# Keys of batch 0 with tokens on partitions, outers from PSUM, beta on 48 rows, d_ff in quarters, and loads placed in the written order

## The chip, the cores and the metric

The kernel runs on one core of one Trainium2 chip. The metric is the device time of an execution in microseconds. A core has five engines that run their own instruction queues in order: TensorE (PE, matmuls, with weight loads listed apart as PEld), VectorE (DVE), ScalarE (ACT), GpSimd (POOL) and SyncE (SP, which here only issues DMAs). All times below are microseconds unless marked otherwise, and positions are counted from the start of the profiled span.

## The reference

Two stages. The first is an attention without softmax over batch 4, heads 4, sequence 1088, head size 32. Each query and key is projected by two 8x32 sketches, and the outer product of the two results is its 64-element feature. The second is a feed-forward layer of 2048 units over all 4352 tokens.

```
phi(x) = outer(S1 x, S2 x)                  # 8 x 8 = 64 features for each token and head
kv  = sum over s of phi(k_s) v_s^T          # 64 x 32 for each batch and head
z   = sum over s of phi(k_s)
x_s = (phi(q_s) kv) / (phi(q_s) z + 1e-6)   # heads side by side: 4352 x 128
h   = x w_in;  g = h * sigmoid(beta * h);  out = g w_out
```

## The kernel before, in words

**Order.** Nothing is scheduled by a planner. Each step is a small function with a short name, and the string `SEQ` lists the names in the order in which they are issued; each engine runs its own part of that list in order. A name in capitals puts the same step on the second engine of its pair (`o01` on GpSimd, `O01` on VectorE; `ca1` on ScalarE, `CA1` on VectorE). `+` issues one wave of the feed-forward layer (`w1`: two 512-column matmuls of xT with w_in units into a two-bank PSUM buffer `wave`, L384, and one silu on ScalarE, L393). `-` issues one accumulation (`w2`: two matmuls with scaled w_out units, L359). `~` is one warming matmul (`keep_warm`, L189) that computes nothing needed. Eleven more of these are issued at the very start. A chunk is 512 tokens and needs 8 waves and 8 accumulations; there are 68 of each in all, the last four with 256 columns in place of 512. `+` is issued only for tokens whose xT has been made.

**PSUM.** `wave` has two buffers of two banks, `two` one buffer of two banks, `one` one bank, and `moeout` one bank. Whoever wants a buffer waits for the last reader of the tile before.

**Batch 0 (the prologue).** k arrives in two loads, with head and 32 groups of tokens on partitions. VectorE turns it in 32x32 blocks (`turn_k`, L420). `kps` projects it with the sketches (L447, 8 matmuls of 288 columns), and `kab` turns the result, so that tokens lie on partitions (L468). `outer` multiplies the two projections to features (L483, in five pieces, `o00` to `o04`), `gram` (L545) with `gram_terms` and `gram_z` makes z, and `kv0` accumulates kv with v (L531). Of q, batch 0 is done in two parts: A (tokens 0 to 511, loaded first) and B (512 to 1087, a later load). `spread` projects q twice, as a (`aa`, `ab`) and b (`ba`, `bb`); `asb` copies a's result out of PSUM (`ca`, `cb`), `mult` multiplies it by b's (`ma`, `mb`). `den0` multiplies by z (`da`), `invert` and `spread_rc` make the reciprocals (`ia`, `ra0`, `ra1`), `num0` makes the numerator (`na`), and `divide0` writes xT (`xa0`, `xa1`, L624).

**Weights.** The silu needs beta times h, so w_in is multiplied by beta (`prep_win`, `u0` to `u3`, 512 columns each, on GpSimd, L308) and w_out divided by it (`prep_rbeta`, L316, and `prep_wout_act`, `w0` to `w7`, L322). beta is first split into three bf16 terms on 12 partitions (`beta_top`, `beta_left`) and broadcast by matmuls with a selector (`beta_half`, L283) and copies (`beta_copy`, L293). A d_ff index is half, partition and unit of eight, so unit j of a half is read from `winp` with a step of 8.

**Batches 1 to 3** follow among the waves: `tk`, `kp`, `ka`, outers, `g` (gram, L636), `gm`, `wz`, `qp`, `qa`, `c`, outers of q (`p10` ...) and their turns (`t10` ...), kv (`va`, `vb`), `np`, and the numerator (`n1`, L721).

**Loads.** All loads but three small ones go through SP's queue. In the kernel before they are issued ahead of everything: k 0, first q 0, v 0 (four loads of 144 KB), both halves of w_in, half of w_out, beta_pu (for `rb`), second q 0, k 1, the other half of w_out, q 1, v 1, k 2, q 2, v 2. At most eight are under way: the ninth after a load waits until that load has landed.

Of the kernel before, what the change touches and what calls it, by code (L numbers as in the profile page):

```python
# [9 lines left out]
F32 = mybir.dt.float32  # L10
# [4 lines left out]
P = 128  # L15
# [3 lines left out]
def kernel(  # L19
# [12 lines left out]
    nc = tc.nc  # L32
# [26 lines left out]
    NU = NJ // 2  # L59
# [25 lines left out]
    def sb(shape, dtype, name):  # L85
        return const.tile(shape, dtype, tag=name, name=name)
# [7 lines left out]
    beta_pu = sb([P, 2, NU], F32, "beta_pu")  # L94
    NB = 3 * 4
    beta_r = sb([NB, DFF // 4], F32, "beta_r")
# [3 lines left out]
    for n, s_ in enumerate((S1, S2)):  # L100
# [10 lines left out]
            ap=[[DFF // 4, 4], [0, 3], [1, DFF // 4]],  # L111
# [16 lines left out]


# [18 lines left out]
    def load_wout(i):  # L148
        nc.sync.dma_start(
            out=w_out_sb[:, NU * i : NU * i + NU, :],  # L150
            in_=bass.AP(
                tensor=moe_w_out.tensor,
                offset=moe_w_out.offset + i * NU * P * P,
                ap=[[NU * P, P], [1, NU * P]],
            ),
        )

    def load_late():
        nc.sync.dma_start(
            out=beta_pu,  # L160
            in_=bass.AP(
                tensor=moe_beta.tensor, offset=moe_beta.offset, ap=[[NU, P], [P * NU, 2], [1, NU]]
            ),
        )

    K_PARTS = ((0, 18), (18, T))
    QA0 = 2 * q_chk[0][1]
    load_rows(k, k_t, 0, "k", K_PARTS)
    load_rows(q, q_t, 0, "q", ((0, QA0),))
    load_v(0)  # L170
    load_win(0, DFF // 2)
    load_win(DFF // 2, DFF)
    load_wout(0)
    load_late()
    load_rows(q, q_t, 0, "q", ((QA0, T),))
    load_rows(k, k_t, 1, "k")
    load_wout(1)
    load_rows(q, q_t, 1, "q")
    load_v(1)
    load_rows(k, k_t, 2, "k")  # L180
    load_rows(q, q_t, 2, "q")
    load_v(2)

# [42 lines left out]
    for n in range(2):  # L226
        qT2.append(sb([P, T, 32], F32, f"qT{n}"))
        kT2.append(sb([P, TPAD, 32], F32, f"kT{n}"))
        nc.gpsimd.memset(kT2[n][:, T:, :], 0.0)
    zb0 = sb([P, H, 32], F32, "zb0")  # L230
# [5 lines left out]
    bsel = sb([NB, 4], BF16, "bsel")  # L236
    bsel4 = sb([NB, 4], F32, "bsel4")
    nc.vector.tensor_reduce(out=bsel4, in_=cut(ident[:NB], [[3, 4], [1, 3]]), op=ADD, axis=AX.X)
# [3 lines left out]
        out=bpos[:, 0:1], in_=cut(ident[:NB], [[3, 4], [1, 2]], 1), op=ADD, axis=AX.XY  # L242
    )
    nc.vector.tensor_reduce(
        out=bpos[:, 1:2], in_=cut(ident[:NB], [[3, 4]], 2), op=ADD, axis=AX.X
# [9 lines left out]
    skc = sk.rearrange("p m n r -> p (m n r)")  # L255
    sab = []


    def prep_s(n):
        st_ = sb([P, 4, R], F32, f"st{n}")  # L260
        nc.vector.transpose(out=st_.rearrange("p u r -> p (u r)"), in_=sr[n])
        nc.gpsimd.tensor_tensor(out=sk[:, :, n, :], in0=st_[:, :2, :], in1=hm, op=MUL)
        t = sb([P, R, R], F32, f"s{n}")
        nc.scalar.copy(out=t, in_=cut(st_, ([[1, R], [0, R]], [[0, R], [1, R]])[n]))
        sab.append(t.rearrange("p i j -> p (i j)"))
# [4 lines left out]
    bq = sb([NB, DFF // 4], BF16, "bq")  # L270
    br = [beta_r, sb([NB, DFF // 4], F32, "br1"), bq]
    bt = sb([NB, DFF // 4], BF16, "bt")
# [7 lines left out]
    def beta_half(i):  # L280
        t = two("betaps")
        for n in range(2):
            nc.tensor.matmul(  # L283
                out=t[:, n],
                lhsT=cut(bsel, [[0, P]], 2 * i + n),
                rhs=bq,
                start=True,
                stop=True,
            )
        PS["beta", i] = t  # L290

    def beta_copy(i):
        nc.scalar.copy(  # L293
            out=beta_bc[:, 1024 * i : 1024 * i + 1024],
            in_=PS["beta", i].rearrange("p a b -> p (a b)"),
        )
# [6 lines left out]
    WP = 512  # L303
# [6 lines left out]
    def win_unit(j):  # L310
        i, u = divmod(j, NU)
        assert all(n in given for n in range(i * NU * P // WP, (i + 1) * NU * P // WP))
        return cut(winp, [[NU, P]], i * NU * P + u)
# [110 lines left out]

    def turn_q(b, t0=0, t1=T):
        nc.vector.transpose(  # L426
            out=qT2[b % 2][:, t0:t1].rearrange("p t s -> p (t s)"),
            in_=q_t[b][:, t0:t1].rearrange("p t d -> p (t d)"),
        )

    PS, KP, QO, QT, QP, ND, KAB, QAB, ASB, KVZ, KVD, RB = ({} for _ in range(12))
# [32 lines left out]

    def turn_ab(t, name):
        o = sbA.tile([P, NJK, H, 2 * R], F32, tag=name, name=name)
        for pi in range(2):
            nc.vector.transpose(out=cut(o, [[2 * R * H, NJK], [1, 32]], 32 * pi), in_=t[:, pi, :JW])  # L468
        return o
# [8 lines left out]
    def outer(dst, b, src, nm, j0, j1, eng=None):  # L478
        if b not in dst:
            dst[b] = sbA.tile([P, NJK, H, F], F32, tag=nm, name=nm, bufs=1)  # L480
        a0 = src[b][:, j0:j1]
        n = H * (j1 - j0)
        (eng or nc.vector).tensor_tensor(  # L483
            out=cut(dst[b][:, j0:j1], [[F, n], [R, R], [1, R]]),
            in0=cut(a0, [[2 * R, n], [1, R], [0, R]]),
            in1=cut(a0, [[2 * R, n], [0, R], [1, R]], R),
            op=MUL,
        )
# [11 lines left out]
    def spread(which, n, dsts):  # L500
        t0, tn = q_chk[n]
        for c in range(2):
            for m in range(2):
                for pr, dst in enumerate(dsts):
# [3 lines left out]
                        out=dst[64 * c : 64 * c + 64, m, : 32 * tn],  # L508
# [231 lines left out]
    def b_A():  # L740
        PS["bA"] = [wave2("bps"), wave2("bps")]
        spread("b", 0, PS["bA"])
# [86 lines left out]
    do("kp0", kps, 0)  # L829
    do("ka0", kab, 0)  # L830
# [23 lines left out]
    for n in range(2):  # L854
        do(f"s{n}", prep_s, n)
        do(f"tk0{n}", turn_k, 0, *K_PARTS[n])
        do(f"be{n}", beta_half, n)
        do(f"bc{n}", beta_copy, n)
# [9 lines left out]
    for n in range(DFF // WP):  # L868
        do2(f"u{n}", prep_win, (n,), POOL, DVE)
    for i in range(NJ // 2):  # L870
        do(f"w{i}", lambda i: [prep_wout_act(j) for j in (2 * i, 2 * i + 1)], i)
    for b in range(1, B):
# [41 lines left out]
        s1 s0 sw bt0 ~ bl0 ~ ~ tk00 tk01 ~ kp0 bt1 tqa aa ca0 ~ ka0 ~ BL1 gr zt ~ o00 ca1 be0 ba o01 ~  # L914
        bc0 O02 ma0 zz v00 ma1 o03 be1 o04 lk3 da ia v01 bc1 v02 v03 ra1 v04 rb kd u1 nd nc u0 ra0 tqb
        na ~ w0 w2 ab w3 cb0 xa0 xa1 u3 + CB1 w1 bb ~ tk1 mb1 ~ + - kp1 w6 + mb0 ka1 u2 + O11 - w7 g1 -
        o12 w4 + tq1 + gm1 wz1 qp1 wm1 db w5 - + nb qa1 c1 ib o13 o10 xb + - - ct1 + CM1 cr1 CD1 - P11 +
        p12 - + va1 t12 p13 vb1 vc1 + p10 + np1 - t11 + - nz1 - - lq3 t13 t10 + n1 x10 tk2 x11 - + kp2 +
        - ka2 - + o23 tq2 - + g2 + lv3 - gm2 wz2 - o21 o22 tk3 wm2 + + c2 qp2 o20 + - + qa2 ct2 CM2 - +
        - - + cr2 - CD2 p21 P20 + - + va2 vb2 t21 + VC2 - + - p22 np2 nz2 t22 - p23 t20 t23 + n2 x20 x21  # L920
        - tq3 + kp3 ka3 O30 + - + - + g3 + gm3 wz3 - o32 + o33 - wm3 + qp3 qa3 + c3 + - + - - + - + ct3
        CM3 o31 cr3 - CD3 + va3 P33 p32 vb3 P30 vc3 + - t33 p31 t30 t31 + np3 t32 NZ3 + - - + n3 - - x30
        x31 + - + - + - + - - + - + - + - + - - + - + - + - - + - + - + - - + - + - + - + - + + - - - -
# [33 lines left out]
```

## Time and profile before

| | |
|---|---|
| runs of the kernel before | 106.12, 106.44, 112.31; median 106.44 |
| profiled execution | 106.56, its span 104.6 |
| busy in the span | PE 96.6 (92%), ACT 82.8 (79%), DVE 57.0 (54%), POOL 36.8 (35%) |
| first wave starts | 17.66 |
| batch 1's gram starts (L636) | 23.85 |
| last silu of 68 ends | about 100.3 |
| wave matmuls (L384), accumulations (L359) | 144 and 144 |

Busy time is the time in which an engine had an instruction in it; matmul ends are modelled, so a TensorE that is busy all through need not be at its peak. The granted clock (PEclk) is a share of TensorE's full speed. "Released by" names what ended a wait. In the chain of work that ended last each entry gives start, length and what it was, and the entries follow on one another without a hole.

### The profile page before, as it was taken

What the parts mean: (1) busy time and instruction counts of PE and PEld (TensorE: products, weight loads), DVE (VectorE), ACT (ScalarE), POOL (GpSimd) and SP (SyncE); (2) the same over time, 40 slices, a digit from 0 to 9 for tenths busy, and PEclk for the clock granted to TensorE, in tenths of its full rate; (3) what the DMA queues carried; (4) which work ended last, traced back from release to release, by engine and by line L of the source; (5) the groups of instructions that cost most, each with busy time, mean ns of one, the idle gap of its engine ahead of it and who ended that gap; (6) DMA issues with size and microseconds to landing.
All of it is one profiled execution on the core that took longest, in us unless ns stands there. A gap on an engine that the chain in (4) does not pass through costs nothing.

```text
span 104.6 us, 2769 instructions
## 1 busy us (share of the span) xinstructions
PE 96.6 (92%) x1143; PEld 50.9 (49%) x1143; DVE 57.0 (54%) x119; ACT 82.8 (79%) x108; POOL 36.8 (35%) x41
## 2 busy tenths in 40 slices
PE   5979975999999999999999999999999999999850
PEld 2424631337246653563565546345755555556730
DVE  4577778957799880963968551589950020110210
ACT  0935539689969988878997799999997999999930
POOL 4249997009504910692095019307500000000000
PEclk9999998599999999999999999999999999999996
DMA  0998999999970580058202400042001506013263
GB/s 8 287 259 235 387 420 345 185 219 305 197 147 23 75 228 19 0 74 200 45 0 33 73 0 0 3 70 34 0 0 27 79 0 100 0 28 50 34 98 50
DMA packets 23084, 11.35 MB, mean 108 GB/s; under 512 B 19220, under 2 KB 21268, under 8 KB 23072
## 3 DMA queue, kind: packets, MB, share of 16 engines
q1 hardware_dynamic: 22368, 11.07, 45.4%
q8 instruction: 9, 0.15, 0.6%
q10 hardware_dynamic: 704, 0.11, 0.6%
q14 instruction: 3, 0.02, 0.1%
HBM read 8.95 MB, written 2.23 MB: 107 GB/s over the span
## 4 chain that ended last, share of the span: by engine, by line
PE 77%; DMA 12%; ACT 3%; SPq 2%; DVE 1%; issue 1%; ACTq 0%
PE wave L384 30%; PE moeout L359 27%; DMA q<-in_q_dram 8%; PE nps L721 4%; DMA v<-in_v_dram 4%; ACT g L393 3%; PE kvz L531 3%; PE gp L636 2%; PE kps L447 2%; PE qps L447 2%; PE cps L678 2%; SPq L120 1%; PE bps L507 1%; DVE qT L426 1%; PE kvz L189 1%
## 5 line engine op out<-in xcount | busy, mean ns | idle before, releaser
L393 ACT ACTIVATE g<-wave 128x1024 f16<-128x1024 f32 x68 | 65.7, 1026 | 7.1 <-PE wave L384 6.7
L384 PE MATMUL wave<-xT,winp 128*128 128x512 f16 (+1 forms) x144 | 41.2, 378 | 0.4 <-ACT g L393 0.3
L359 PE MATMUL moeout<-g,woutp 128*128 128x512 f16 (+1 forms) x144 | 38.1, 367 | 0.0
L384 PEld LDWEIGHTS <-winp 128*128 128x128 f16 x144 | 19.4, 146 | 15.1 <-issue 4.9
L483 POOL TENSOR_TENSOR kp<-kab 128x512 f32<-128x512 f32 (+2 forms) x14 | 17.1, 1250 | 19.3 <-DVE kab L468 13.3
L359 PEld LDWEIGHTS <-woutp 128*128 128x128 f16 x144 | 13.7, 99 | 13.1 <-issue 2.3
L369 DVE STREAM_TRANSPOSE o_sb<-moeout 128x512 f32<-128x512 f32 (+1 forms) x9 | 6.2, 686 | 24.3 <-PE moeout L359 24.3
L483 POOL TENSOR_TENSOR qo<-qab 128x512 f32<-128x512 f32 (+1 forms) x8 | 11.4, 1449 | 14.7 <-DVE qab L701 14.7
L494 DVE STREAM_TRANSPOSE qt<-qo 128x512 f32<-128x512 f32 (+1 forms) x12 | 8.6, 751 | 0.6 <-POOL qo L483 0.5
L189 PE MATMUL kvz<-idle 128*128 128x384 f16 x22 | 6.3, 427 | 1.1 <-DVE idle L98 1.1
L468 DVE STREAM_TRANSPOSE kab<-kps 128x288 f32<-128x288 f32 x8 | 3.3, 456 | 6.3 <-PE kps L447 6.3
L420 DVE STREAM_TRANSPOSE kT<-k 128x1088 f32<-128x1088 f32 (+2 forms) x5 | 5.4, 1072 | 1.2 <-DMA k<-in_k_dram 1.2
L322 ACT ACTIVATE woutp<-w_out_sb,rbeta 128x128 f16<-128x128 f32 x16 | 5.2, 394 | 1.0 <-DVE rbeta L316 1.0
L426 DVE STREAM_TRANSPOSE qT<-q 128x1088 f32<-128x1088 f32 (+2 forms) x5 | 5.3, 1067 | 0.4 <-DMA q<-in_q_dram 0.3
L531 PE MATMUL kvz<-kp,v 128*32 128x64 f32 x288 | 5.0, 220 | 0.0
L308 POOL TENSOR_TENSOR winp<-w_in_sb,beta_bc 128x512 f16<-128x512 f32 x4 | 5.0, 1271 | 0.2 <-DMA w_in_sb<-in_moe_w_in_dram 0.2
L531 PEld LDWEIGHTS kvz<-kp,v 128*32 128x32 f32 x288 | 4.4, 110 | 1.3 <-issue 0.8
L732 ACT CAST xT<-nps 128x576 f16<-128x576 f32 x6 | 3.8, 638 | 1.3 <-PE nps L721 1.2
L721 PE MATMUL nps<-qt,nd 32*32 32x288 f32 x192 | 4.8, 412 | 0.0
L189 PEld LDWEIGHTS <-idle 128*128 128x128 f16 x22 | 2.4, 120 | 4.9 <-issue 3.6
L468 DVE STREAM_TRANSPOSE qab<-qps 128x288 f32<-128x288 f32 x6 | 2.5, 461 | 3.2 <-PE qps L447 3.2
L447 PE MATMUL kps<-kT,sk 64*32 64x288 f32 x64 | 3.5, 414 | 0.5 <-DVE kT L420 0.5
(87 smaller groups left out, 70.0 us busy)
## 6 DMA issues: line engine op xcount, KB each, us to landing
v<-in_v_dram SPq DMA_DIRECT2D x15, 144.0 KB, 4.9
k<-in_k_dram SPq DMA_DIRECT2D x3, 544.0 KB, 9.3
q<-in_q_dram SPq DMA_DIRECT2D x3, 544.0 KB, 11.7
out_dram<-o_sb SPq DMA_DIRECT2D x20, 64.0 KB, 2.0
w_in_sb<-in_moe_w_in_dram SPq DMA_DIRECT2D x2, 512.0 KB, 8.5
w_out_sb<-in_moe_w_out_dram SPq DMA_DIRECT2D x2, 512.0 KB, 9.6
k<-in_k_dram SPq DMA_DIRECT2D x1, 288.0 KB, 2.9
q<-in_q_dram SPq DMA_DIRECT2D x1, 288.0 KB, 8.8
```

The source lines that it names most:

```text
L189: nc.tensor.matmul(out=kvz0[:, P:], lhsT=idle, rhs=cut(idle, [[0, 3], [1, P]]), start=fresh, stop=True, skip_group_check=True,)
L359: nc.tensor.matmul(out=moe["acc"][:, :tw], lhsT=woutp[:, j, :], rhs=g[jj], start=(j == 0), stop=(j == NJ - 1),)
L369: nc.vector.transpose(out=o_sb[:, :nt, :].rearrange("p t d -> p (t d)"), in_=moe["acc"][:, :tw])
L384: nc.tensor.matmul(out=wv[:, jj // per, o : o + tw], lhsT=win_unit(j0 + jj), rhs=xT[:, t0 : t0 + tw], start=True, stop=True,)
L393: nc.scalar.activation(out=g[:, :, :gw], in_=wv[:, :, :gw], func=ACTF.Silu)
L426: nc.vector.transpose(out=qT2[b % 2][:, t0:t1].rearrange("p t s -> p (t s)"), in_=q_t[b][:, t0:t1].rearrange("p t d -> p (t d)"),)
L447: nc.tensor.matmul(out=t[32 * g : 32 * g + 32, pi, :JW], lhsT=skc[rows, :], rhs=moving(rows, g), start=True, stop=True,)
L468: nc.vector.transpose(out=cut(o, [[2 * R * H, NJK], [1, 32]], 32 * pi), in_=t[:, pi, :JW])
L483: (eng or nc.vector).tensor_tensor(out=cut(dst[b][:, j0:j1], [[F, n], [R, R], [1, R]]), in0=cut(a0, [[2 * R, n], [1, R], [0, R]]), in1=cut ...
L494: nc.vector.transpose(out=QT[b][:, j0:j1].rearrange("p j h c s -> p (j h c s)"), in_=QO[b][:, j0:j1].rearrange("p j h f -> p (j h f)"),)
L531: nc.tensor.matmul(out=KVZ[b][32 * h : 32 * h + 32, :F], lhsT=v_t[b][:, h, j, :], rhs=KP[b][:, j, h, :], start=(j == 0), stop=(j == NJK - ...
L721: nc.tensor.matmul(out=tiles[g // 2][32 * h : 32 * h + 32, g % 2, :JW], lhsT=ND[b][rows, fc, 32 * h : 32 * h + 32], rhs=QT[b][rows, :, h, ...
```

## The change

It has five parts.

1. *Keys of batch 0.* VectorE turns k's blocks into `kTm`, where each of nine columns of blocks holds four groups of 32 tokens (groups start at 0, 9, 18, 26). One matmul per column, with 128x128 of `kTm` as weights and a wide sketch `skw` of 64 columns, gives the projections with tokens on partitions (`kp0`, in two parts of four and five matmuls, the first in a `one` buffer, the second in a `two` buffer). `ka0` copies them out, the first part on VectorE and the second on ScalarE. v of batch 0 is loaded with the same groups.
2. *Outers.* The one outer on VectorE reads its left input from PSUM; the copy serves the right one and GpSimd. In the new order that is `O01`, and `o00`, `o02`, `o03`, `o04` go to GpSimd.
3. *beta* is split on 48 partitions with 128 columns, not on 12 with 512, and broadcast in four parts.
4. *d_ff in quarters.* Units are read with a step of 4; w_in and beta are handled by quarters, and w_in comes in three loads (256, 256 and 512 KB). A wave needs its own quarter only. Both spreads of q's part A share one `wave` buffer pair (columns 0 and 256).
5. *Order.* Loads behind the first q are names in `SEQ` (`lv`, `lb`, `lqb`, `lo`, `lw`, `lk`, `lq`): v 0, beta_pu and the second q 0 come first, then w_out's first half, a quarter of w_in, k 1, a quarter, half of w_in, q 1, the other half of w_out, v 1, q 2, v 2, k 2. `SEQ` is new throughout; `~` stands in it five times instead of eleven, and some steps change engines.

```diff
-    NU = NJ // 2
+    NU = NJ // 4
+    CB = P
...
-            ap=[[DFF // 4, 4], [0, 3], [1, DFF // 4]],
+            ap=[[CB, NJ], [0, 3], [1, CB]],
...
+    def load_v0(g):
...
+        nc.sync.dma_start(
+            out=v_t[0][32 * g : 32 * g + 32],
+            in_=bass.AP(
+                tensor=v.tensor,
+                offset=v[0, 0].offset + GS[g] * D,
+                ap=[[T * D, 32], [S * D, H], [1, NJK * D]],
...
+    GS = (0, 9, 18, 26)
...
-    load_v(0)
-    load_win(0, DFF // 2)
-    load_win(DFF // 2, DFF)
-    load_wout(0)
-    load_late()
-    load_rows(q, q_t, 0, "q", ((QA0, T),))
-    load_rows(k, k_t, 1, "k")
...
+    kTm = sb([P, NJK, P], F32, "kTm")
...
+    def prep_sk():
+        for n in range(2):
+            nc.gpsimd.tensor_tensor(out=sk[:, :, n, :], in0=STT[n][:, :2, :], in1=hm, op=MUL)
...
+        nc.gpsimd.tensor_tensor(out=skw[:, :, n, :], in0=st_, in1=cut(gm, [[1, H], [0, R]]), op=MUL)
...
+    def beta_part(i):
+        t = PS["beta", i] = two("betaps")[:, 0]
+        for n in range(NU):
             nc.tensor.matmul(
+                out=t[:, CB * n : CB * n + CB],
+                lhsT=cut(bsel, [[0, P]], NU * i + n),
                 rhs=bq,
...
+    def turn_k0(n):
+        for g0, g1, nj in (((0, 2, NJK),), ((2, 4, NJK - 1),))[n]:
+            o = GS[g0]
+            nc.vector.transpose(
+                out=cut(kTm, [[32, g1 - g0], [P, nj], [1, 32]], 32 * g0),
+                in_=k_t[0][:, o : o + nj * (g1 - g0)].rearrange("p t d -> p (t d)"),
+            )
...
+    KH = 4
...
+    def kp0(j0, j1):
+        n = int(j0 >= KH)
+        KPS[n] = two("kabp")[:, 0] if n else one("kabp")
+        for j in range(j0, j1):
+            nc.tensor.matmul(
+                out=KPS[n][:, kcol(j) : kcol(j) + 64],
+                lhsT=kTm[:, j],
+                rhs=skw.rearrange("p h n r -> p (h n r)"),
...
+    def ka0(j0, j1, eng):
...
+        eng(
+            out=KAB[0][:, j0:j1].rearrange("p j h c -> p (j h c)"),
+            in_=KPS[int(j0 >= KH)][:, kcol(j0) : kcol(j1 - 1) + 64],
+        )
...
+        left = cut(a0, [[2 * R, n], [1, R], [0, R]])
+        if b == 0 and eng is nc.vector:
+            left = cut(KPS[int(j0 >= KH)], [[2 * R, n], [1, R], [0, R]], kcol(j0))
...
     def b_A():
-        PS["bA"] = [wave2("bps"), wave2("bps")]
-        spread("b", 0, PS["bA"])
+        PS["bA"] = [t[:, :, 256:] for t in PS["A"]]
+        spread("b", 0, PS["A"], 256)
...
     SEQ = """
-        s1 s0 sw bt0 ~ bl0 ~ ~ tk00 tk01 ~ kp0 bt1 tqa aa ca0 ~ ka0 ~ BL1 gr zt ~ o00 ca1 be0 ba o01 ~
-        bc0 O02 ma0 zz v00 ma1 o03 be1 o04 lk3 da ia v01 bc1 v02 v03 ra1 v04 rb kd u1 nd nc u0 ra0 tqb
-        na ~ w0 w2 ab w3 cb0 xa0 xa1 u3 + CB1 w1 bb ~ tk1 mb1 ~ + - kp1 w6 + mb0 ka1 u2 + O11 - w7 g1 -
...
+        s0 lv00 ~ ~ lv01 ~ bt0 s1 tk00 tk01 tqa kp00 bl0 bt1 lv02 kp01 bl1 KA00 aa ba ka01 be0 gr bc0
+        be1 lv03 O01 lb CA1 o00 o02 ca0 o03 ma1 lqb zt bc1 v00 ma0 sw lo0 rb o04 v01 v02 be2 bc2 zz be3
+        bc3 v03 v04 tqb da kd ~ nd lw0 lk1 lw1 nc na ia ra0 ra1 w3 lw2 lq1 u0 ab w0 xa0 xa1 cb0 lo1 ~
+        cb1 sk + w1 bb tk1 u1 + w2 - kp1 u2 u3 + mb1 mb0 ka1 - + o13 g1 + - tq1 gm1 + wz1 wm1 w6 o12 qp1
+        db + qa1 w4 + nb ib o11 c1 ct1 w7 o10 lv1 - cm1 xb cr1 lq2 CD1 - va1 lv2 vb1 w5 p12 lk2 VC1 + +
+        - - - + np1 p13 + lk3 - t12 + t13 p11 p10 NZ1 t11 t10 - lq3 - + - - + n1 x10 x11 + - tk2 tq2 kp2
...
```

## The prediction

> **What bounds the kernel now.** I read the rows of slices first (the span in 40 slices of 2.6 us, busy share in tenths, and the granted TensorE clock):
>
> ```profile
> PE   5979975999999999999999999999999999999850
> ACT  0935539689969988878997799999997999999930
> POOL 4249997009504910692095019307500000000000
> PEclk9999998599999999999999999999999999999996
> ```
>
> From the eighth slice (18 us) to the 37th TensorE is full; before that it has holes, and in slices 7 and 8 its clock falls. So the span is a prologue, a body bound by TensorE, and a short tail. The chain that ended last says the same, and names what ends the prologue (start, length, what):
>
> ```profile
> 7.28 8.79 DMA q<-in_q_dram
> ...
> 16.08 0.79 DVE qT L426
> ...
> 16.92 0.75 PE aps L507 x16
> 17.66 1.03 PE wave L384 x2
> 18.69 1.19 PE bps L507 x16
> 19.89 0.75 PE kvz L189 x2
> 20.64 0.69 PE wave L384 x2
> ```
>
> The first wave starts at 17.66. The load of the second part of q (issued 7.28, landed 16.06) releases it. In the body a pair of 512-column matmuls takes 0.43; here the first takes 1.03, because the clock is halved. VectorE's timeline shows the same end from its side:
>
> ```profile
> 15.44 0.25 DVE L316 RECIPROCAL rbeta<-beta_pu 128x16 f32<-128x16 f32 x1 [0.63 <-DMA beta_pu<-in_moe_beta_dram]
> 15.61 0.39 DVE L604 STREAM_TRANSPOSE rb<-rc 128x256 f32<-128x256 f32 x1
> 16.08 0.78 DVE L426 STREAM_TRANSPOSE qT<-q 128x576 f32<-128x576 f32 x1
> 16.79 0.71 DVE L624 TENSOR_TENSOR xT<-nps,rb 128x256 f16<-128x256 f32 x2
> ```
>
> xT's first 512 tokens, which the first wave reads, are finished at 17.50. VectorE could have made them 1.4 us sooner: 0.63 it waits for beta_pu and 0.78 it turns the late part of q, both queued ahead of L624.
>
> For the clock I asked for busy time by stretches of 3.41 us, the length of the half-clock stretch:
>
> ```profile
> 3.97:7.38 3.41, 2.49 (x24) 0.83 (x22) 2.35 (x4) 1.97 (x6) 1.34 (x2) 1.00 1.01 286
> 7.38:10.80 3.42, 3.42 (x56) 1.54 (x56) 2.70 (x5) 1.84 (x3) 2.76 (x3) 1.00 0.98 249
> 10.80:14.21 3.41, 3.02 (x100) 2.15 (x99) 2.58 (x6) 1.70 (x4) 3.21 (x4) 1.00 1.02 394
> 14.21:17.62 3.41, 1.84 (x34) 0.53 (x35) 2.54 (x7) 2.13 (x7) 3.41 (x3) 1.00 1.03 406
> 17.62:21.03 3.41, 3.41 (x28) 1.15 (x23) 3.01 (x4) 2.24 (x4) 0.07 (x1) 0.50 1.08 192
> ```
>
> The second column is TensorE's busy time, the third from the right the clock. After a stretch with 1.84 busy the clock is 0.50 for one stretch; after 2.49 it stays at 1.00. So the limit lies between 1.84 and 2.49.
>
> **The body moves as a block.** From batch 1's gram (L636, at 23.85, when 4 waves and 2 accumulations have been issued) TensorE is full until 94.6. Its work from there is the same after the change, and the new order reaches batch 1's gram with the same counts (4 and 2). So the sum is: how much earlier does that gram start?
>
> **The change part by part.**
>
> *Keys.* Removed: 8 projections of batch 0 (L447, 2 x 0.69, the first from 5.33) and two turns of kab (L468, 0.81 together). Added: nine matmuls with 128x128 f32 weights and 64 columns, two instructions each, 18 in all. No row has this form. Lower end: the 18 of the old gram (L545) took 0.77. Upper end: L657's two f32 loads of 128 columns took 0.41, 0.205 each, so 3.7. I take L545's pitch, 0.77/18 = 0.043, plus what 64 more weight columns add to a load:
>
> ```profile
> L545 PEld LDWEIGHTS gram<-kab 128*64 128x64 f32 x18 | 0.7, 137 | 0.3 <-issue 0.3
> ...
> L657 PEld LDWEIGHTS gp<-gmz,s2w 128*128 128x128 f32 x6 | 1.1, 189 | 0.4
> ```
>
> that is 0.053, so 0.096 each and 1.75 us for all. They need all of k turned (6.25), so nothing can start at 5.33 any more: 6.33 to 8.1. VectorE's turns of k keep their sizes (576 and 512 columns, 0.78 and 0.71). The copies of the products cost 0.43 on VectorE (256 columns, as L802) and about as much on ScalarE.
>
> *Outers.* The one on VectorE reads one input from PSUM: 0.68 (L524, which reads PSUM so, took that beside a busy GpSimd) where the old one took 1.44. The next gram shares its bank and waits for it, with the beta parts and kv behind; VectorE ends it at 8.4, before TensorE gets there. GpSimd has three outers of 1.12 and one of 0.62, about 7.7 to 12.0; kv's end waits for that in either kernel.
>
> *Beta.* The splits run on 128 columns instead of 512: 0.72 becomes about 0.27 on ScalarE (a 128-column copy, L768) and 1.15 at most 0.62 on GpSimd (256 columns). They were not on the path. The broadcast is four parts of 0.30 on TensorE and 0.54 on ScalarE, the same in total; each waits for the copy before it, since the buffer is single.
>
> *Second projections of q, spread b.* They write the same banks as spread a and wait for no copy, but the copies now wait for both spreads (0.69 later).
>
> *Loads.* SP issues one more (0.43, it idles then). The queue delivers in order: v has landed by about 9, beta_pu and q's second part come right behind (0.3 MB), at 10 to 11 instead of 15.4 and 16.06. Both are wanted on VectorE after 11.5: hidden, and the cost if 2 us late is 1 for 1. The first quarter of w_in now has 2.44 MB up to its end, as w_in's second half had, which landed at 13.9; GpSimd's 1.25 makes it 15.2. First wanted at 16.6: hidden by 1.4. k of batch 1 is wanted at 16 to 18 and has 2.98 MB; in the kernel before, 2.92 MB had landed by 15.4. SP's stores come later than all of these but the last two loads.
>
> *Quarters of d_ff.* Weights are read with a step of 4, not 8. The load (0.146) lies under 0.216 of matmul: nothing, unless it passes 0.216.
>
> *Other moves.* `s2_wide` (0.29) now stands ahead of the last outer on GpSimd and is in the 12.0; the scalings of w_out come in another order, under waves as before.
>
> *Warming matmuls.* Five single ones remain of eleven. One fewer ahead of the keys, 0.16 less.
>
> **The clock decides.** Up to 7.38 the new kernel has 0.95 of warming matmuls (1.11 less 0.16) and 1.05 of keys from 6.33: 2.0 busy, between 1.84 (lost) and 2.49 (kept), and nearer to lost. I take it as lost: half clock from 7.38 to 10.80. (The old L507 group took 1.26 at half clock, 0.69 at full.) Then on TensorE: keys to 8.8, spread a to 10.05, spread b to 11.1, beta part 0 11.4, gram 12.15, part 1 12.45, kv 13.1, part 2 13.4, zz 14.0, part 3 14.3, kv 14.7, den 15.35. VectorE, with the late waits gone: invert 1.36 (as 12.98 to 14.34), two spreads 0.8, two divides 0.7. First wave at 18.1, at full clock, since 14.21 to 17.62 is then busy for about 3.
>
> From there: the copies of spread a's second part are both on ScalarE, and spread b waits for them (19.0); ScalarE's first silu follows; second wave 20.0, accumulation, keys of batch 1 behind `mb1` on VectorE at 20.9, third wave 21.5 (its buffer waits for `mb0`), gram at 22.8. Against 23.85: **1.05 gained**. The tail, bound by ScalarE (silus end to end from 80.75), loses one copy of 0.64 to VectorE; TensorE itself is 1 us from full there, so I count 0.3. The four outers of q in batch 1 all go to GpSimd (5.8 us, was 4.1): numerator 1 waits 0.65 for them, which is within the lead that batch 1 has by then. Sum: 106.56 - 1.05 - 0.3 = 105.2 for the profiled execution (span 104.6, 1.96 around it). That execution stands 0.12 over the median of the runs, 106.44, so **105.0**.
>
> **Rivals.**
> 1. *The clock stays up.* The keys then end at 8.1, den at 13.7, first wave 16.6, gram 21.4, 2.45 earlier: 103.7. For it: 2.0 is over 1.84. Against: it is far under 2.49. Chance 0.25. [...]
> 2. *Slower: the key matmuls don't overlap their weight loads.* At 0.205 each, 3.7 us, the keys end at 11.75, spread b at 13.1 instead of 11.1: 107.0. It passes the old time from 0.17 us per instruction on. For it: L657's two loads stand 0.2 apart. Against: L545's 18 do not. Chance 0.15.
> 3. *The body has holes.* Numerator 1, 2 or 3 waits for outers and turns by more than the lead: 1 to 1.5 us given back, 106.3. For it: GpSimd's longer chain. Against: TensorE has other waves to do. Chance 0.1. That the loads don't come sooner (q's part still at 16) belongs here: first wave near 17.7, about 105.5 to 106.
>
> **How the numbers follow.** Forecast 0.5 (104.2 to 105.8 on its own). The range, 103.2 to 107.0, leaves out the better half of rival 1 and the worst of rival 2. Two per cent, about what a measurement here tells from no change, is 2.1 us: faster means under 104.3. That holds in most of rival 1 and a fifth of the forecast: 0.33; slower than 108.6 needs rival 2 and a second loss: 0.07; the rest 0.60.
>
> **What would show it.** The clock row: 0.5 in slice 4 and partly in 3 and 5, full in 7 and 8. The key matmuls' busy time near 1.75. q's turn not waiting for a load. First wave at 18.1, gram of batch 1 at 22.8, TensorE full from there. Wrong if the clock falls elsewhere, if the first quarter of w_in lands after 16, or if TensorE shows holes after 25 us.

## The result and the profile after

The changed kernel takes **110.58** (median of four executions: 109.64, 109.77, 111.39, 112.30), the kernel before 106.28 beside it (105.84 to 112.31). The ratio is **1.032, 95% interval 1.024 to 1.040**: slower. The forecast was 105.0, with a range of 103.2 to 107.0, so both the size and the sign were wrong. (Executions more than 1.5% above a kernel's fastest are left out of its ratio, here and below, so a ratio can differ from the quotient of the medians.)

The profiled execution took 109.77, its span 108.0. The rows of slices (2.7 us each), answering to those of before:

```profile
PE   6959999899999999999999999999999999999850
ACT  2701533599988897999989869999993999999920
POOL 5319888001952790097279800007000000000000
PEclk9996555589999999999999999999999999999999
```

The TensorE row is nearly full from the fourth slice on (the eighth before). The last row is what went wrong: the clock is at half in four slices and in parts of two more, where before it was in one and a part of another. The stretches of 3.41 us of the same execution (columns: start and end, length, then busy time and instructions of TensorE, its weight loads, VectorE, ScalarE and GpSimd, then granted clock, DMA share and GB/s):

```profile
5.24:8.65 3.41, 2.32 (x20) 2.05 (x18) 2.58 (x5) 0.17 (x1) 0.82 (x2) 1.00 1.11 247
8.65:12.07 3.42, 3.42 (x54) 2.05 (x53) 1.37 (x3) 1.12 (x3) 3.33 (x5) 0.50 1.04 346
12.07:15.48 3.41, 3.41 (x74) 2.78 (x74) 2.08 (x5) 1.36 (x3) 2.64 (x5) 0.50 1.04 408
15.48:18.89 3.41, 3.36 (x48) 1.83 (x48) 0.59 (x2) 1.23 (x5) 3.02 (x3) 0.50 1.05 334
18.89:22.31 3.42, 3.11 (x35) 0.83 (x35) 2.95 (x7) 2.15 (x7) 0.00 (x0) 0.50 1.06 258
22.31:25.72 3.41, 3.19 (x40) 1.29 (x39) 1.70 (x4) 3.31 (x7) 0.00 (x0) 1.00 1.09 224
```

Four stretches at half clock, 8.65 to 22.31, with TensorE busy for 3.42, 3.41, 3.36 and 3.11 of 3.41. A TensorE that is busy all through did not bring its clock back here. Its timeline shows what that did to the prologue (start, length, what; in brackets the idle time ahead and what ended it):

```profile
6.63 2.23 PE L487 MATMUL kabp<-skw,kTm 128*128 128x64 f32 x18 [1.09 <-DVE kTm L433]
8.80 2.01 PE L548 MATMUL aps<-qT,s 32*64 32x256 f32 x32
...
13.01 1.51 PE L572 MATMUL kvz<-kp,v 128*32 128x64 f32 x48
...
20.23 1.26 PE L548 MATMUL aps<-qT,s 32*64 32x288 f32 x16
21.43 0.50 PE L189 MATMUL kvz<-idle 128*128 128x384 f16 x1
21.72 0.89 PE L389 MATMUL wave<-xT,winp 128*128 128x512 f16 x2
...
26.83 0.77 PE L677 MATMUL gp<-kab 128*64 128x32 f32 x18
```

The first wave starts at 21.72 (17.66 before), batch 1's gram at 26.83. In the same view of the kernel before that gram stands at 23.78:

```profile
23.78 0.77 PE L636 MATMUL gp<-kab 128*64 128x32 f32 x18
```

From the gram to the end of the execution it is 82.94 here and 82.78 there. So the body did move as a block, to 0.16, and all else of the loss lies ahead of that gram. VectorE, which named the end of the prologue before, now waits for TensorE:

```profile
13.60 0.24 DVE L321 RECIPROCAL rbeta<-beta_pu 128x16 f32<-128x16 f32 x1
13.76 0.72 DVE L439 STREAM_TRANSPOSE qT<-q 128x576 f32<-128x576 f32 x1
18.26 0.45 DVE L635 STREAM_TRANSPOSE dT<-dps 128x256 f32<-128x256 f32 x1 [3.78 <-PE dps L624]
```

The two loads that it waited for in the kernel before are no longer waited for; in their place it waits 3.78 for the denominators, which TensorE makes at half clock.

### The profile page after: what moved, and what is told of

Same layout as the page of the kernel before. It is cut to its first block, busy times and chain, and to the rows that moved or that the text cites. A ratio compares the mean times of both kernels' runs of the same rounds, so it can differ in the third digit from the quotient of the medians.

```text
span 108.0 us, 2812 instructions
## 1 busy us (share of the span) xinstructions
PE 100.9 (93%) x1151; PEld 51.7 (48%) x1151; DVE 54.4 (50%) x118; ACT 81.0 (75%) x107; POOL 36.4 (34%) x48
## 3 DMA queue, kind: packets, MB, share of 16 engines
HBM read 8.95 MB, written 2.23 MB: 103 GB/s over the span
## 4 chain that ended last, share of the span: by engine, by line
PE 84%; ACT 5%; DMA 3%; SPq 1%; issue 1%; DVE 1%; ACTq 0%
PE wave L389 28%; PE moeout L364 26%; PE kvz L572 5%; PE nps L762 4%; ACT g L398 4%; DMA k<-in_k_dram 3%; PE aps L548 3%; PE kabp L487 2%; PE betaps L293 2%; PE gp L677 2%; PE kps L460 2%; PE qps L460 2%; PE cps L719 2%; PE nps L653 2%; PE dps L624 1%
## 5 line engine op out<-in xcount | busy, mean ns | idle before, releaser
L389 PE MATMUL wave<-xT,winp 128*128 128x512 f16 (+1 forms) x144 | 40.4, 372 | 0.6 <-ACT g L398 0.5
L389 PEld LDWEIGHTS <-winp 128*128 128x128 f16 x144 | 15.2, 116 | 17.0 <-issue 6.5
L524 POOL TENSOR_TENSOR kp<-kab 128x512 f32<-128x512 f32 (+2 forms) x14 | 15.5, 1130 | 16.2 <-DVE kab L506 13.7
L524 POOL TENSOR_TENSOR qo<-qab 128x512 f32<-128x512 f32 (+1 forms) x9 | 10.7, 1216 | 15.0 <-DVE qab L742 15.0
L189 PE MATMUL kvz<-idle 128*128 128x384 f16 x16 | 5.5, 511 | 1.1 <-DVE idle L99 1.1
L572 PE MATMUL kvz<-kp,v 128*32 128x64 f32 x288 | 6.0, 244 | 0.0
L302 ACT COPY beta_bc<-betaps 128x512 f32<-128x512 f32 x4 | 2.3, 586 | 4.5 <-PE betaps L293 4.5
L773 ACT CAST xT<-nps 128x576 f16<-128x576 f32 x4 | 2.6, 639 | 2.0 <-PE nps L762 2.0
L506 DVE STREAM_TRANSPOSE kab<-kps 128x288 f32<-128x288 f32 x6 | 2.5, 462 | 2.7 <-PE kps L460 2.7
L425 DVE STREAM_TRANSPOSE kT<-k 128x1088 f32<-128x1088 f32 x3 | 3.8, 1280 | 0.0
```

The lines of the kernel that those rows point to most:

```text
L189: nc.tensor.matmul(out=kvz0[:, P:], lhsT=idle, rhs=cut(idle, [[0, 3], [1, P]]), start=fresh, stop=True, skip_group_check=True,)
L389: nc.tensor.matmul(out=wv[:, jj // per, o : o + tw], lhsT=win_unit(j0 + jj), rhs=xT[:, t0 : t0 + tw], start=True, stop=True,)
L524: (eng or nc.vector).tensor_tensor(out=cut(dst[b][:, j0:j1], [[F, n], [R, R], [1, R]]), in0=left, in1=cut(a0, [[2 * R, n], [0, R], [1, R]] ...
L572: nc.tensor.matmul(out=KVZ[b][32 * h : 32 * h + 32, :F], lhsT=v_t[b][:, h, j, :], rhs=KP[b][:, j, h, :], start=(j == 0), stop=(j == NJK - ...
```

## The experiments

A warming matmul (`~`) is work whose result nobody reads.

### Does the clock explain the loss? Warming matmuls ahead of the keys

`after_fill`: eight `~` more, ahead of the key projections, in TensorE's wait for k.

```diff
-        ... tk00 tk01 tqa kp00 bl0 bt1 lv02 kp01 ...
+        ... tk00 tk01 tqa ~ ~ ~ ~ ~ ~ ~ ~ kp00 bl0 bt1 lv02 kp01 ...
```

> The changed kernel with eight more warming matmuls in the hole of TensorE ahead of the key matmuls (5.5 to 6.6). Theory 1 (the clock is the loss, and the hole starts it): the clock stays up past 8.65; if the busy prologue then holds it, the first wave starts near 17 and the time is 104 to 105. Theory 2 (the clock is the loss, but small f32 matmuls alone don't hold it, the warming matmuls between them did): the clock falls one stretch of 3.4 later, 107.5 to 109. Theory 3 (the new order itself is longer, whatever the clock): no gain, 109.5 to 110.5.

Measured: 106.86 (105.00 to 107.56), ratio 0.999 (0.993 to 1.005); by the medians it is still 0.8 above the kernel before (106.02 beside it), and above the 104 to 105 expected if the clock is the loss. Instructions that compute nothing take 3.7 us off. The profiled execution (106.05) has a full clock from 3.90 on, with batch 1's gram at 23.07, 3.76 before that of the changed kernel. So without the four stretches at half clock the gram comes 3.76 sooner, 0.94 for each, and that is net of a stall of 0.88 that the changed kernel does not have (below). What is left stands near the old time, not 2.7 below it as the rival with a full clock had it; the timeline shows where that went:

```profile
6.50 2.19 PE L487 MATMUL kabp<-skw,kTm 128*128 128x64 f32 x18 [0.31 <-DVE kTm L433]
...
15.68 0.45 PE L548 MATMUL aps<-qT,s 32*64 32x288 f32 x1
17.00 0.74 PE L548 MATMUL aps<-qT,s 32*64 32x288 f32 x15 [0.88 <-issue]
...
17.85 0.59 PE L389 MATMUL wave<-xT,winp 128*128 128x512 f16 x2
...
23.07 0.77 PE L677 MATMUL gp<-kab 128*64 128x32 f32 x18
```

The keys take 2.19 where I had 1.75, and TensorE stands for 0.88 inside one group of matmuls, waiting for nothing that the profile shows ("issue"; more on that at the end).

`after_warm`: nine more on top of these, spread over the prologue, so that every stretch is well filled.

```diff
-        ... KA00 aa ba ka01 be0 gr bc0
+        ... KA00 aa ~ ba ~ ka01 be0 gr ~ bc0
-        ... bc2 zz be3
-        bc3 v03 v04 tqb da kd ~ nd lw0 lk1 lw1 nc na ia ...
+        ... bc2 zz ~ be3
+        bc3 v03 v04 tqb ~ da kd ~ ~ nd lw0 lk1 lw1 nc ~ ~ na ~ ia ...
```

> The same with nine warming matmuls more, spread through the prologue (after spread a, spread b, gram, zz, the last kv, ahead of and behind nd and na). Theory 1 and theory 2: full clock through the prologue, first wave at 17 to 17.5, time 103.7 to 105. Theory 3: each warming matmul costs its 0.16 on top, 110 to 111.

Measured: 107.07 (106.82 to 107.15), ratio 1.010 (1.004 to 1.016), which none of the three theories had. The clock is full from 5.62 on, all four executions lie within 0.33, and the nine, some 1.5 in all, put off the first wave by 1.54 and the gram by 1.13 (19.39 and 24.20, against 17.85 and 23.07).

### The warming matmuls alone

`before_5warm`: the kernel before with five single `~` in place of eleven.

```diff
-        ... tk00 tk01 ~ kp0 bt1 tqa aa ca0 ~ ka0 ~ BL1 gr zt ~ o00 ca1 be0 ba o01 ~
-        ... u3 + CB1 w1 bb ~ tk1 mb1 ~ + - kp1 ...
+        ... tk00 tk01 kp0 bt1 tqa aa ca0 ka0 BL1 gr zt o00 ca1 be0 ba o01
+        ... u3 ~ + CB1 w1 bb tk1 mb1 + - kp1 ...
```

> The kernel before with five single warming matmuls instead of eleven, placed as the changed kernel has them (three ahead of the keys, one near the numerator, one ahead of the first wave). Theory 2: the clock falls in the prologue and the kernel before becomes slower, 108 to 110. Theory 1: its keys start at 5.3 and leave no hole, so it keeps the clock to 14 and stays at 106 to 106.5. Theory 3: 105.5 to 106.3, since six matmuls are gone.

Measured: 108.23 (107.38 to 108.90), ratio 1.024 (1.016 to 1.031). Its stretches:

```profile
3.84:7.25 3.41, 2.40 (x22) 0.73 (x20) 1.49 (x2) 2.10 (x6) 1.44 (x3) 1.00 1.02 271
7.25:10.67 3.42, 1.91 (x39) 1.07 (x40) 2.47 (x6) 1.07 (x2) 1.25 (x1) 1.00 1.01 267
10.67:14.08 3.41, 3.41 (x51) 1.79 (x50) 2.00 (x3) 1.18 (x2) 3.41 (x5) 0.50 1.05 399
14.08:17.50 3.42, 3.03 (x66) 2.06 (x65) 2.00 (x6) 1.28 (x2) 3.42 (x3) 0.50 1.03 405
```

Fewer warming matmuls alone cost 2.2 us (106.02 beside it), with two stretches lost in the profiled execution (107.38); by their mean clocks of 0.952 the three others lost three. The last two lines also break my reading of the clock: the stretch with 3.41 busy was followed by half clock, the one with 3.03 by full clock. So the granted clock does not go by busy time in these lines (I call gate whatever sets it).

`before_hold`: the kernel before with four `~` more behind `na`, to fill the stretch that lost the clock in the profile of before.

```diff
-        na ~ w0 w2 ab w3 cb0 ...
+        na ~ ~ ~ ~ ~ w0 w2 ab w3 cb0 ...
```

> The kernel before with four warming matmuls more, behind the numerator, in the hole where TensorE waits for the late part of q (15.7 to 16.9). If the gate counts array work, the stretch from 14.2 goes from 2560 to 4096 full columns and the half-clock stretch behind it goes: first wave near 17.5 at full clock, 105.0 to 105.6. If the start of the waves is held by something else by then (instructions arriving, silus): 106 to 106.5.

Measured: 107.75 (107.01 to 111.03), ratio 1.011 (1.006 to 1.017): slower by about 1%, and outside both expectations. In the profiled execution (111.03) the first part of q landed late (spread a waited 1.95 for it), so that an earlier stretch (6.58, with 1.46 busy) lost the clock and the three behind it were at half, at 3.42, 3.41 and 3.02 busy. Whether the four held the clock where they stand can't be read from it. The three other executions have mean clocks of 1.000, 0.995 and 0.995, too high for a lost stretch (one takes 0.016 off the mean), and still took 107.01 to 107.95. But ten of the thirteen executions of the kernel before beside it have 0.992 and more as well: the stretch lost in the profile of before is not lost in most executions, and there was little to hold. The cost of a place fixed on one profile shows all the same.

### What does the gate count?

I counted the array work of each stretch from the trace's matmul rows: columns streamed, times the weights' rows x columns over 128 x 128, an f32 instruction counted twice (an assumption), an instruction across a boundary shared out by its length. The fullest stretch of the fourteen profiles holds 8,120. Some stretches of several kernels, those nearest to the limits among them:

| clock in it | kernel, start | TensorE busy | array work | next stretch |
|---|---|---|---|---|
| half | changed, 8.65 | 3.41 | 2,760 | half |
| half | changed, 12.07 | 3.41 | 2,110 | half |
| half | changed, 15.48 | 3.36 | 2,640 | half |
| half | changed, 18.89 | 3.11 | 3,210 | full |
| half | before_5warm, 10.67 | 3.41 | 1,650 | half |
| half | before_5warm, 14.08 | 3.03 | 3,000 | full |
| half | before, 17.62 | 3.41 | 3,650 | full |
| half | before_keys (below), 3.68 | 3.07 | 3,060 | half |
| half | before_keys, 24.16 | 3.41 | 3,020 | full |
| full | before_5warm, 7.26 | 1.91 | 1,700 | half |
| full | before, 14.20 | 1.84 | 2,690 | half |
| full | changed, 5.24 | 2.33 | 2,630 | half |
| full | after_narrow (below), 5.02 | 3.41 | 2,630 | full |
| full | after_oldkeys (below), 9.63 | 3.19 | 2,720 | full |
| full | after_fill, 14.14 | 2.18 | 2,860 | full |
| full | after_oldkeys, 6.21 | 2.05 | 3,020 | full |

By busy time the rows don't sort: 2.05 and 2.18 kept the clock, 2.33 lost it; 3.41 stayed at half, 3.03 was released. By array work they nearly do, and so do all 404 whole stretches of the fourteen profiles. A full clock was lost up to 2,690 and kept from 2,630 on (about a third of 8,120). A half clock was not released up to 2,760, and was from 3,000 on; the exceptions are the first two stretches of `before_keys`, 3,050 and 3,060, not released, and the one in the tail of before (99.54), where the clock was lost with 2,870. Counted without the share of the array the stretches don't sort (17,720 columns lost the clock in before, 14.20; 5,510 kept it in after_narrow, 5.02), nor with f32 counted once (1,510 was released in before_5warm, 14.08; 1,610 was not in changed, 15.48). How far the count can be trusted: shared out from each start to the next, a row moves by up to some 200, and the order next to the limits changes. (The boundaries of `before_keys` are carried back by steps of 3.413 from 27.58, its first record.)

`after_narrow` was meant to test it: the eight `~` of `after_fill` use 32 x 32 of the array in place of 128 x 128, in the same time each.

```diff
+    def keep_narrow(n):
+        for _ in range(n):
+            nc.tensor.matmul(out=kvz0[:32, P:], lhsT=idle[:32, :32], rhs=cut(idle[:32], [[0, 3], [1, P]]), ...)
```

> The changed kernel with eight narrow warming matmuls in the hole ahead of the keys: the same 384 columns, but on 32 rows and 32 columns of the array, so as long and a sixteenth of the array work. If the gate counts the time in which TensorE is busy: as with the eight full ones, 106 to 107.5. If it counts array work (columns streamed times the share of the array in use, where the traces so far put the limit between 2752 and 2816 full columns in 3.41 us): the hole adds 192 instead of 3072, the clock falls as in the changed kernel, 109.5 to 111.5.

Measured: 106.08, 106.54, 111.12 and 113.00: not settled. In the profiled execution (106.54) the stretches fell so that the clock was kept at 2,630; in two others the time is that of a lost clock (the mean clock shows it for 111.12, with 0.915, and not for 113.00, with 0.992). `after_fill` with wide ones had none above 107.56.

The second try stands where the verdict is clearer, in the half-clock part itself. `after_mid_wide` adds two `~` on each side of spread b in the changed kernel, `after_mid_narrow` the same with 32 x 32.

```diff
-        ... KA00 aa ba ka01 be0 gr bc0
+        ... KA00 aa ~ ~ ba ~ ~ ka01 be0 gr bc0
```

> The changed kernel with four warming matmuls of 128 x 128 x 384 added in the half-clock part, two on each side of the second projection of q (at about 11 us). Theory work: the stretch from 8.65 to 12.07 had 2,760 columns of full array, and with the four it has about 3,260, over the 2,930 to 3,080 at which other stretches were released, so the clock is back at 12.07 instead of 22.31; 10.2 us at half clock become 5 to 7, less 1.3 for the four: 107 to 108.5. Where the phase of the stretches differs, less. Theory busy: that stretch was busy for 3.41 of 3.41 and was not released, so the four only cost their 1.28 at half clock: 111.5 to 112.

> As the run before, but the four use 32 x 32 of the array in place of 128 x 128 (384 columns each, the same time). Theory work: they add a sixteenth of the work each and push other work out of the stretch, so the clock comes back no sooner than in the changed kernel: 111 to 112.5. Theory busy: the same time as the run before. If the gate counts columns whatever the share of the array, also the same as the run before.

Measured (an execution's half-clock stretches are worked out from its mean clock and span: (1 - clock) x span / (0.5 x 3.41); a clock that was not yet released at the start does not show in it):

| kernel | executions: time (half-clock stretches) | median |
|---|---|---|
| after_mid_wide | 106.80 (0.1), 106.96 (0.1), 107.33 (0.2), 108.56 (1.0), 108.60 (1.0), 108.62 (1.0), 108.94 (1.0), 110.57 (2.3), 110.91 (4.0), 113.35 (6.5) | 108.61 |
| after_mid_narrow | 107.13 (0.2), 111.06 (4.5), 111.20 (4.5), 113.21 (6.5) | 111.13 |

Busy time would make the two equal. They aren't: with wide matmuls the commonest outcome is one half-clock stretch, with narrow ones more than four, as in the changed kernel (109.77: 4.1; 109.64: 4.0). The medians, 108.61 and 111.13, stand just above and inside what array work gave (107 to 108.5, 111 to 112.5); busy time gave 111.5 to 112 for both. Only four executions stand on the narrow side, and three of ten wide ones lost two stretches and more, so these two runs alone could be chance. In the rows above the clock does not follow busy time (3.41 was followed by half and by full); that it follows array work is a reading of the count over all profiles, with these runs and `after_narrow` on its side. An exact limit is not shown. The profiled executions (106.80 and 107.13) are both of the kind that kept the clock and say nothing here.

### Which part of the change loses the clock?

`after_oldkeys`: the changed kernel with batch 0's keys, their copies, outers and v's groups as before; order, loads, beta, quarters and the five `~` are those of the change.

```diff
-        ... tk00 tk01 tqa kp00 bl0 bt1 lv02 kp01 bl1 KA00 aa ba ka01 be0 gr bc0
+        ... sk tk00 tk01 tqa kp0 bl0 bt1 lv02 bl1 ka0 aa ba be0 gr bc0
```

> The changed kernel with batch 0's keys, kab, outers and v groups as in the kernel before (projected by L447's form, turned on VectorE, the VectorE outer from SBUF); order, loads, beta and quarters stay. If the late start of the keys (6.6 instead of 5.3) cost the clock: it holds, 106 to 107.5. If the missing warming matmuls did: these keys do half the array work of the new ones (1152 against 2304 full columns), the clock falls as before or earlier, 109.5 to 112.

Measured: 106.00 (104.79 to 106.30, and 109.73 and 109.93, with four half-clock stretches each), ratio 0.991 (0.987 to 0.996). One part taken back, and the loss is gone in eight of ten executions, where all four of the changed kernel had it; the rest of the change is worth 0.6 (the medians) to 0.9 (the ratio).

`before_keys`: the opposite, the kernel before with the new keys and outers alone, eleven `~` kept.

```diff
-        ... tk00 tk01 ~ kp0 bt1 tqa aa ca0 ~ ka0 ~ BL1 gr zt ~ o00 ca1 be0 ba o01 ~
+        ... tk00 tk01 ~ kp00 kp01 bt1 tqa KA00 ka01 aa ca0 ~ ~ o00 O01 BL1 gr zt ~ ca1 be0 ba o02 ~
```

> The kernel before with the first two parts alone: keys with tokens on partitions, one outer read from PSUM, v in the same groups; its order and its eleven warming matmuls stay. The clock should hold to 14 as in the kernel before. Theory of the prediction, sizes only: keys end 0.8 later than the old ones, the outer saves 0.7 on VectorE, 106 to 107. If the keys cost the clock by themselves: 108 to 110.

Measured: **114.32** (113.52 to 116.33), ratio 1.073 (1.067 to 1.078), far beyond both expectations. Two rows of TensorE's timeline:

```profile
6.38 4.08 PE L492 MATMUL kabp<-skw,kTm 128*128 128x64 f32 x18 [0.34 <-DVE kTm L438]
...
31.19 0.77 PE L682 MATMUL gp<-kab 128*64 128x32 f32 x18
```

The same 18 instructions take 4.08 in place of 2.23. The clock was never released in the prologue: its first record is "full" at 27.58, and the half clock that the executions start with lasted until then (in the trace of before the warming matmuls start 0.32 apart up to 3.91 and 0.16 apart behind the first record, at 3.96). The profile prints this as a mean clock of 1.000, since there is no record ahead of the release; the mean must be read with the lengths of known instructions beside it.

`before_keys_fill`: eight `~` added to it, ahead of the keys.

```diff
-        ... tk00 tk01 ~ kp00 kp01 bt1 ...
+        ... tk00 tk01 ~ ~ ~ ~ ~ ~ ~ ~ ~ kp00 kp01 bt1 ...
```

> The kernel before with the new keys and outers alone (which gave 114.3, at half clock up to 27.6), and eight warming matmuls of 384 columns added ahead of the keys. Theory work: the stretch from 3.7 to 7.1 gains about 900 columns of full array, the clock is released there or one stretch later, and what is left is the price of the keys themselves and of the warming matmuls: 106.5 to 108.5. Theory busy: TensorE was busy for 3.07 and then 3.41 of 3.41 in the stretches of the half clock and was not released, so more busy time changes nothing: 114 to 116.

Measured: 106.41 (105.97 to 106.71), ratio 1.000 (0.997 to 1.003).

```profile
7.04 2.12 PE L492 MATMUL kabp<-skw,kTm 128*128 128x64 f32 x18
...
23.24 0.77 PE L682 MATMUL gp<-kab 128*64 128x32 f32 x18
```

Eight instructions without use bring the gram from 31.19 to 23.24 and the time from 114.3 to 106.4. At full clock the new keys cost nothing and bring nothing; the 8 us were the clock's. What they do to the array work can be read from the counts: they can't start before all of k is turned (6.38 to 6.63, where the old projections start at 5.33), so that the array stands idle or needs filling until then, and at half clock their 18 x 64 columns, counted twice, are 2,300 in 4.08, or 1,930 in a stretch, under the 2,760 that was not released in the changed kernel. The three stretches behind them, from 10.51 to 20.75, hold about 2,640, 1,570 and 2,700 (an estimate from the rows of TensorE's timeline), no more than that either.

### The loads alone

`before_loads`: the kernel before with beta_pu and the second part of q issued right behind v, as the change does.

```diff
     load_v(0)
+    load_late()
+    load_rows(q, q_t, 0, "q", ((QA0, T),))
     load_win(0, DFF // 2)
     load_win(DFF // 2, DFF)
     load_wout(0)
-    load_late()
-    load_rows(q, q_t, 0, "q", ((QA0, T),))
```

> The kernel before with beta_pu and the second part of q loaded right behind v, nothing else changed. If the loads were worth what the prediction gave them: VectorE waits for neither, first wave at 16.3 to 16.9, time 104.8 to 105.8. If another queue is as late (w_in then lands 0.3 MB later and GpSimd makes two quarters of it before the first wave): 106 to 106.5.

Measured: 106.25 (105.09 to 112.39), ratio 0.998 (0.993 to 1.002): no difference that can be told. In the profiled execution, the best of the ten (105.09, clock full from 6.46 to the tail), the first wave starts at 16.54 and the gram at 22.22, both over 1 us sooner than before. Then comes this:

```profile
16.54 0.41 PE L384 MATMUL wave<-xT,winp 128*128 128x512 f16 x1
17.68 0.38 PE L384 MATMUL wave<-xT,winp 128*128 128x512 f16 x1 [0.73 <-issue]
```

The first wave is split by a stall of 0.73, the same kind as in `after_fill`. The loads do take the wait away that ended the prologue (the first wave starts 1.12 sooner), and 0.73 comes back as the stall.

### The earlier keys with six more warming matmuls

`oldkeys_warm`: `after_oldkeys` with five `~` in the hole behind the key projections and one behind batch 0's gram.

```diff
-        ... kp0 bl0 bt1 lv02 bl1 ka0 aa ba be0 gr bc0
+        ... kp0 ~ ~ ~ ~ ~ bl0 bt1 lv02 bl1 ka0 aa ba be0 gr ~ bc0
```

> The changed kernel with the earlier form of batch 0's keys (as in the comparison that gave 106.0 and 0.991), and six warming matmuls of 384 columns added: five in TensorE's hole of 1.37 us behind the key projections (7.16 to 8.53), one behind batch 0's gram. Theory work (the clock of a stretch of 3.41 us is kept by the columns streamed times the share of the array that they use; counted from the matmul rows of all kernels, stretches with 2,620 and less lost the clock and stretches with 2,701 and more kept it): without the six, a stretch that begins between 4.5 and 7.0 holds 1,540 to 2,700, so that the clock falls in some executions (109.7 and 109.9 among the ten), and with them at least 3,000: no execution above 107, median 105.5, ratio 0.985 to 0.99. Theory busy (busy time alone keeps the clock): the same sign, since the hole is filled to 0.6 of 1.37. Theory other (the 109.7 and 109.9 have another cause): still two or three of ten executions near 109.8, median 106.2.

Measured: 105.80 (105.12 to 107.09, eleven of twelve at 106.05 and below), ratio 0.994 (0.991 to 0.996), beside 106.51 for the kernel before, which reached 112.54. The two outcomes near 110 of `after_oldkeys` did not come in twelve executions, which may in part be chance, and the gain, 0.7, is small: the ratio falls short of the 0.985 to 0.99 expected, though its interval stays below 1. The time lies 4.8 below the median of the change.

## Why the prediction was wrong, step by step

The forecast for the profiled execution was 105.2; it took 109.77, 4.57 more. Of these 4.10 are the gram (26.90 in the chain of waits that the forecast used, 22.8 predicted), 0.3 the tail's gain, which did not come, and 0.16 a body slightly longer.

- **The step that failed is "half clock from 7.38 to 10.80", one stretch.** That the clock would fall in the keys' stretch was right, but by luck: I had 2.0 busy in the stretch from 3.97, it was 2.33 in the one from 5.24, and 2.05 and 2.18 kept the clock elsewhere. That it would be back one stretch later, since TensorE would be busy, was not: it came back after four. I took the limit from five stretches of one profile and read it as busy time. The profile of before could have warned me: a busy stretch followed by full clock (17.62, 3.41) has wide waves in it (3,650 of array work), while the work that I listed behind the keys is all narrow, spreads of 32 x 64, kv of 128 x 32, a gram of 128 x 64. By their mean clocks (0.935 and 0.936) the executions of 109.77 and 109.64 lost four stretches each. Those of 111.39 and 112.30 have 0.998 and 0.993, and no trace shows where their time went; a clock that was not released at the start, as in `before_keys`, would print so.
- **The phase** was taken as that of before (3.97). The stretches do not begin at one place: in these profiles the first release lies between 3.84 and 6.58 (27.58 in `before_keys`). The stretch that decided here began at 5.24, not at 3.97. So a place "just filled" in one profile is a matter of chance in the next execution. The kernel before is not safe either: six of 29 executions beside the last runs took 110.34 to 112.54, with mean clocks of 0.923 and 0.937, which is four or five stretches at half clock.
- **Keys, 18 x 0.096, taken as 1.75, from 6.33** (the product is 1.73; in the same way 105.2 less 0.12 is 105.1, and the forecast said 105.0): 2.23 from 6.63, that is 0.124 each; at full clock 2.12 to 2.19. The weight loads fill 2.08 of it, 0.116 each, so they seem to set the pace. My step from L545 to 128 columns of weights was 0.02 to 0.03 short for each instruction. The rival that had 0.205 each is out.
- **Full clock, 103.7 (rival 1):** `after_fill` shows it to be 106.05 (105.00 in the best execution). Its gram stands at 23.07 where I had 21.4: 0.17 from k, 0.44 from the keys, 0.88 from the stall and 0.42 between the first wave and the gram (5.22 for 4.80), less 0.24 made good elsewhere. That TensorE is busy in a half-clock stretch did not bring the clock back by itself: 3.41 busy of 3.41 was followed by another 0.50 three times in the stretches quoted above, and 3.36 once.
- **Loads:** right. beta_pu landed at 9.9 (10 to 11 forecast), and q's turn and `rbeta` wait for nothing (13.76 and 13.60). Seen alone, the step gains nothing measurable (0.998).
- **Outer from PSUM, copies, beta, quarters, w_in:** sizes as forecast (0.69 for 0.68; copies 0.41 and 0.43; beta copies 0.59 for 0.54), none of them on the path; `u0` runs from 12.71 to 13.99, sooner than the 15.2 that I allowed.
- **Body as a block:** right to 0.16; rival 3, holes, did not happen. **Tail 0.3:** not seen; the distance from gram to end is the same with one ScalarE copy less.
- **The range** ended at 107.0, with one mishap beside the forecast. The clock had been priced at one stretch or none, though in a prologue of narrow work they were lost in a row (four in the changed kernel, three in `before_hold`, two in `before_5warm`): that outcome had no place among my cases.

## What to carry to other kernels

Ask of every stretch of 3.41 us how much of the array its matmuls use, not how long TensorE is busy: here stretches with 1,650 to 2,760 columns stayed at half clock at 3.36 to 3.41 busy, and ones with 3,000 to 3,650 were followed by full clock at 3.03 to 3.41 busy (3,050 and 3,060 in `before_keys` were not). With small or thin matmuls behind a lost clock it stayed lost for four stretches here, and a few warming matmuls of full width ahead of them were worth 3.7 us here and 8 in another order. Before a cheaper form takes the place of early work on TensorE, ask what held the clock there. An early gain in a prologue must be looked for again right behind the place where it arises (of 1.12 in `before_loads` 0.73 came back as a stall), and a median over executions says more than one profile, because the stretches began at different places (first release at 3.84 to 6.58 here).

## What the runs showed of the hardware

**The granted clock.** In the traces of before and after each record of the clock that ends inside the execution lasts 3.413 us or a multiple of it (13.653, 81.920, 85.333); the first begins at 3.96 and 5.24, with full clock. Ahead of it the warming matmuls start 0.32 apart, in the full clock behind it 0.16 (before, 1.35 to 3.91 and 4.10 to 4.75). By the count above, of 8,120 columns in the fullest stretch, a full clock was kept in stretches from 2,630 on and lost in stretches up to 2,690, in the tail of before at 2,870; a half clock was followed by full from 3,000 on and by half up to 2,760, in `before_keys` at 3,050 and 3,060. A row moves by up to some 200 with the way of counting, and whether the clock goes by anything else is open.

**A stop of TensorE near its 221st matmul.** In seven of the traces TensorE stops near its 221st matmul row, at whatever work stands there (the first wave in `before_loads`, the spread of q's second part in the others), and the profile gives "issue" as what ended the wait:

| kernel | TensorE goes on | stall |
|---|---|---|
| after_fill | 17.00 | 0.88 |
| before_loads | 17.68 | 0.73 |
| after_oldkeys | 16.93 | 0.31 |
| after_mid_wide | 17.80 | 0.61 |
| after_mid_narrow | 18.15 | 0.98 |
| oldkeys_warm | 16.84 | 0.72 |
| after_narrow | 17.54 | 1.24 |

In `after_fill` the DMA engines are full with loads in that time, and one packet of another queue, which the profile calls "instruction", moves among them. The view of DMA traffic of `after_fill` from 14.5 to 17.1 (queue and kind: packets, MB, share of the engines):

```profile
q1 hardware_dynamic: 323, 1.01, 99.2%
q8 instruction: 1, 0.02, 2.6%
```

The same view of before from 15.2 to 17.8 has one such packet too, beside loads at 101.6%, and its TensorE, with the first wave at 17.66, does not stop near that row. No run moved the packet or thinned the loads around it, so what TensorE waits for in these stops is not shown.
